# Chunk 0's triangular inverse made from 16x16 blocks joined on TensorE, in a DeltaNet and SiLU feed-forward kernel

## The chip, the cores and the metric

The kernel runs on one core of a Trainium2 chip. The metric is the device time of one execution in microseconds (us). The compute engines are PE (TensorE; its weight loads are shown apart as PEld), DVE (VectorE), ACT (ScalarE) and POOL (GpSimd); SP starts most of the DMAs. Each engine works through its own queue in order.

## What is computed

The reference is a DeltaNet recurrence per batch and head, followed by a two-layer network with SiLU. Everything is float32; batch 4, 8 heads, 768 tokens, head size 48, feed-forward size 2048.

```python
k_n = k / (norm(k) + 1e-6)
for t in range(S):
    y[:, :, t] = einsum('bhd,bhde->bhe', q[:, :, t], state)
    v_old = einsum('bhde,bhd->bhe', state, k_n[:, :, t])
    state = state + beta_t * einsum('bhd,bhe->bhde', k_n[:, :, t], v_t - v_old)
x = y.transpose(0, 2, 1, 3).reshape(3072, 384)
h = x @ w_in                      # 384 x 2048
out = (h * sigmoid(h)) @ w_out    # 2048 x 384
```

## The kernel before

The 768 tokens are cut into six chunks of 128 tokens (`c`), each into two halves of 64 (`hf`). All 32 (batch, head) pairs of a chunk are worked on together, in two groups of two batches (`g`). Within a half, the token-by-token recurrence becomes matrix work: scores between keys, a triangular matrix that has to be inverted, and products with the state.

For each chunk, `turn` (L395) transposes keys (`j` = 0) or negated queries (`j` = 1) on PE into `kq`, `score` (L418) multiplies them into `ap`, and `block_out` and `block_in` (L461, L472) send the 32x32 diagonal blocks of the key scores to DRAM and read them back as `g`, one block per partition: 4 quarters of the chunk times 32 pairs fill the 128 partitions. `norm_steps` (L328) makes the key norms and the factors that `block_steps` (L372) turns into the table `step`.

`invert` (L480) then inverts the 128 triangular blocks on DVE. For m from 31 down to 1 it forms a rank-1 term and adds it: two operations in each of 31 rounds, 62 in all, over 31 to 256 elements in a partition. For chunk 0 (`by_rows`), ACT scales finished rows and turns part of the result while DVE goes on. The result `x`, and half of it transposed (`low`), go to DRAM, from where `xe` and `xi` are read in the layout that `merge` needs, one pair's rows on 32 partitions. `merge` (L556) joins two 32x32 inverses to a 64x64 one with 32x32 matmuls. `solve` (L716) goes on with `keys`, `inner`, `update`, `old` and `new`: products with keys, states, values `vf` and queries, which write the layer input `xT` and the state (L632). Chunk 0's first half has no state yet and takes `first_outputs` (L640) with a slab in `sums_of_w`.

The feed-forward part (`feed_forward`, L913) for a half chunk is `hidden` (L764: 8 steps of f, two column tiles each; PE L771, SiLU on ACT L781) and, for chunk 0, `project` (L794, PE L801). From chunk 1 on `combine` (L855) does the second product with seven half-size products (PE L867), with sums of halves of the weights (`sum_w`) and of the activations (`sum_g`, L851); DVE adds partial results to the output tile (L875).

The weights arrive as float32 words that `narrow` (L176) rounds to a short form before use. There are 16 pieces, eight of `w_in` and eight of `w_out`, 768 KB each. Each takes two ACT operations (L180, L181), then on DVE a maximum (L185), a shift and mask (L188) and a combination with the sign (L192), and an add on POOL (L196). `w_in` pieces are 3 rows of 256 elements in a partition, `w_out` pieces 2 of 384. Raw pieces are parked in tiles not yet in use: `w_outs`, `sums_of_w`, `sums_of_g`, buffers of `gT`.

No scheduler decides the order: `pin` (L78) keeps each engine's instructions in the order in which the code emits them, and `in_line` (L88) does so for SP's DMAs. `run` (L1069) emits the next step of the feed-forward part (first narrowing, with `until`, whatever that step needs), `fill` (L942) the next narrowing step, and `go` the next step of another generator. `busy` (L281) emits matmuls whose result nobody uses (`pw`).

Around the change the order is: keys of chunk 0 loaded, turned, scored, blocks out and back; then queries and weights loaded; chunk 0's inversion on DVE with the query work of chunk 0, key turning of chunk 1 and the first narrowing ACT steps beside it (L1013 to L1033); scaling of V by the norms and masking of the query scores on DVE (L389, L1037); turning of chunk 1's queries (L408); then `solve(0)` with `fill` between its steps, the second half of chunk 0 together with the first hidden pass, `prepare(1)`, and chunk 1's inversion with narrowing and projection between its operations (L1152 to L1156). From there on the loop over chunks 1 to 5 solves a chunk, loads and prepares the next one and inverts its blocks, with feed-forward steps between.

Of the kernel before, what the change touches and what calls it, by code (L numbers as in the profile page):

```python
# [10 lines left out]
FP32 = mybir.dt.float32  # L11
# [10 lines left out]
def kernel(  # L22
# [13 lines left out]
    P = 128  # L36
# [131 lines left out]
    for hf in range(2):  # L168
        in_line(nc.sync.dma_start(out=beta_fm[BH // 2 : BH, :, 1 - hf], in_=of_beta[1][:, :, hf]))
    w_in = const.tile([P, NKT, DFF], FP32, name="w_in")  # L170
# [5 lines left out]
    def narrow(to, raw):  # L176

        low, high = raw[..., 0], raw[..., 1]
        bits = to.bitcast(U32)
        pin(nc.scalar.activation(out=to, in_=high.bitcast(FP32), func=ACTF.Abs))  # L180
# [5 lines left out]
            out=to, in0=to, scalar1=LOW_HIGH, scalar2=None, op0=ALU.max  # L186
        ))
        yield pin(nc.vector.tensor_scalar(  # L188
            out=bits, in0=bits, scalar1=3, scalar2=0x3FFFFFFF,
# [31 lines left out]

    def spare_w(i):
        return sums_of_w[i].rearrange("p f m -> p (f m)").bitcast(U32)

    def fetch_w_in(i):
        if i < 4:
            raw = room(1 - i // 2, i % 2)
        elif i == 4:
            raw = spare_w(2)
        elif i < NWI - 1:  # L230
            raw = mlp.tile([P, SIZE], U32, name="raw", tag="gT", bufs=3)[:]
        else:
            raw = spare
# [8 lines left out]
    def fetch_w_out(i):  # L242
        raw = (
            room(1, 0), room(1, 1), spare_w(1), spare_w(0), spare_w(2), room(1, 1), spare, spare_w(1)
# [31 lines left out]
    for j in range(NB):  # L276
        rows = slice(T * j, T * (j + 1))
        pin(nc.gpsimd.tensor_copy(out=pick[rows], in_=ident[rows, rows]))
    xis = [const.tile([P, HH, W], FP32, name=f"xi{i}") for i in range(2)]
# [48 lines left out]
    def norm_steps(c):  # L328
# [25 lines left out]
        for j in range(NB):  # L354
            rows = slice(T * j, T * (j + 1))
            yield pin(nc.vector.scalar_tensor_tensor(
                out=spread[rows, place(j), :], in0=r[rows], scalar=-1.0, in1=t[rows],
# [8 lines left out]
    def place(j):  # L366

        return 2 * (1 - j % 2) + j // 2
# [14 lines left out]
    def size(c, g):  # L383
# [4 lines left out]
        engine = nc.vector if c == 0 else nc.gpsimd  # L388
        pin(engine.tensor_tensor(out=vf, in0=vf, in1=of, op=ALU.mult))  # L389
# [60 lines left out]
    def block_room(c):  # L450

        blocks[c] = (
            tc.dram_tile([P, T, T], FP32, name=f"blocks{c}"),
            work.tile([P, T, T], FP32, name="g", tag="g", bufs=1),
            work.tile([P, T, T], FP32, name="x", tag="x", bufs=1),
        )
        x = blocks[c][2]
        pin(nc.gpsimd.memset(x[:], 0.0))
        pin(nc.gpsimd.memset(x[:].rearrange("p s t -> p (s t)")[:, 0 : T * T : T + 1], 1.0))

    def block_out(c, g):  # L461

        there, ap = blocks[c][0], aps[c, g]
        for j in range(NB):
            rows, cols = slice(T * j, T * (j + 1)), slice(T * (j % 2), T * (j % 2 + 1))
            at = T * place(j) + HH * g
# [5 lines left out]
    def block_in(c):  # L472
        there, g, _ = blocks[c]
        in_line(nc.sync.dma_start(out=g[:], in_=there[:]))
# [5 lines left out]
    def invert(c, step, by_rows):  # L480
# [3 lines left out]
        if by_rows:  # L484
            low = w_in[:, 0, DFF - T * T : DFF].rearrange("p (t s) -> p t s", t=T)
        else:
            low = g

        def turn_rows(engine, s):
            engine(low[EVEN, :, s], x[EVEN, s, :].rearrange("p s t -> p t s"))  # L490

        def scale_rows(s):
            n = s.stop - s.start
            pin(nc.vector.tensor_tensor(
                out=x[:, s], in0=x[:, s],
                in1=step[:, s].unsqueeze(2).to_broadcast([P, n, T]), op=ALU.mult,
            ))

        K = T // 4
        for m in range(T - 1, 0, -1):  # L500
# [8 lines left out]
            if by_rows and m >= K:  # L509
                pin(nc.scalar.activation(  # L510
                    out=x[:, m, m:T], in_=x[:, m, m:T], func=ACTF.Copy, scale=step[:, m : m + 1]
                ))
                if m in (T // 2, K):
                    turn_rows(by_act, slice(m, 2 * m))
# [707 lines left out]
```

## Time and profile before

| | us |
|---|---|
| median of 3 runs | 790.88 |
| lowest and highest run | 786.69, 790.92 |
| profiled execution | 791.45 |
| its span from first to last instruction | 789.70 |
| PE busy | 710.0 |
| PEld busy | 611.6 |
| DVE busy | 414.0 |
| ACT busy | 201.4 |
| POOL busy | 79.0 |

Busy time is a sum over the span; the same number can hide a stage in which an engine is full and one in which it stands still. So the profile is read by stage. A line such as L504 is a line of the code above; "out<-in" names the tiles; `x62` counts records (a float32 matmul of PE leaves two). "[1.68 <-DMA w]" gives idle time of the engine before the instruction and what ended it. PEclk is the TensorE clock that was granted, as a share of full speed. A list of waits gives the waiting operation, what it waited for, the time in total, how many times and the longest.

### The profile page before, as it was taken

How to read it: one execution, taken by the hardware profiler on the slowest of the kernel's cores; microseconds unless marked ns; L12 is line 12 of the kernel's file. 1: busy time of each engine (PE TensorE's matmuls, PEld its weight loads, DVE VectorE, ACT ScalarE, POOL GpSimd, SP SyncE). 2: the span in 40 equal slices, each digit the busy share in tenths (PEclk: the TensorE clock that was granted, in tenths of full speed). 3: DMA queues.
4: the chain of work that ended last, by engine and by line, in shares of the span. 5: the costliest groups of instructions: out<-in, count | busy, mean ns of one | idle time of the engine just before them, and what ended most of it. 6: DMA issues, size and time to landing. Idle time of an engine off the chain costs nothing.

```text
span 789.7 us, 19980 instructions
## 1 busy us (share of the span) xinstructions
PE 710.0 (90%) x8762; PEld 611.6 (77%) x8762; DVE 414.0 (52%) x969; ACT 201.4 (26%) x423; POOL 79.0 (10%) x82
## 2 busy tenths in 40 slices
PE   5667679688998999998989999989999989999997
PEld 3445566357767888997878998888997978989997
DVE  5868957994503395542395543495443494321212
ACT  2544235203202303212302213202213203222020
POOL 5002514300000100100100100100102000000000
PEclk9579889879999999999999999999999999999999
DMA  5997337004006704018504018404017204010000
GB/s 100 250 149 243 120 79 153 35 21 82 12 21 85 101 1 92 14 30 99 86 0 94 14 29 105 80 22 81 10 28 89 54 21 81 11 29 5 21 1 21
DMA packets 155655, 50.75 MB, mean 64 GB/s; under 512 B 141216, under 2 KB 148512, under 8 KB 155568
## 3 DMA queue, kind: packets, MB, share of 16 engines
q1 hardware_dynamic: 151200, 48.42, 32.7%
q10 hardware_dynamic: 4368, 1.05, 0.7%
q8 instruction: 69, 1.13, 0.6%
q14 instruction: 18, 0.15, 0.1%
HBM read 34.70 MB, written 12.58 MB: 60 GB/s over the span
## 4 chain that ended last, share of the span: by engine, by line
PE 54%; DVE 20%; DMA 9%; issue 2%; ACT 2%; SPq 1%; POOL 0%; DVEq 0%; ACTq 0%
PE phid L771 18%; PE px L867 8%; PE py L867 7%; DVE rank L504 7%; DVE x L515 6%; PE pa L428 3%; PE pyc L681 3%; DMA z<-in_q_dram 3%; PE po L801 3%; PE ph L595 2%; PE pz L607 2%; PE pu L627 2%; PE pyc L668 2%; DMA g<-blocks 2%; PE pt L402 2%
## 5 line engine op out<-in xcount | busy, mean ns | idle before, releaser
L771 PE MATMUL phid<-xT,w_in 128*128 128x256 f32 x1152 | 270.6, 389 | 4.5 <-ACT gT L781 2.8
L771 PEld LDWEIGHTS phid<-xT,w_in 128*128 128x128 f32 x1152 | 217.4, 193 | 40.4 <-issue 3.8
L781 ACT ACTIVATE gT<-phid 128x512 f32<-128x512 f32 x96 | 57.2, 597 | 219.9 <-PE phid L771 213.3
L504 DVE SCALAR_TENSOR_TENSOR rank<-g,step,x 128x31 f32<-128x31 f32 (+15 forms) x186 | 74.6, 401 | 31.2 <-DMA g<-blocks 25.9
L515 DVE TENSOR_TENSOR x<-x,rank 128x31 f32<-128x31 f32 (+15 forms) x186 | 68.3, 367 | 6.8
L867 PE MATMUL py<-w_out,sums_of_g 128*128 128x192 f32 x320 | 58.9, 337 | 7.9 <-DVE o L875 7.9
L867 PEld LDWEIGHTS py<-w_out,sums_of_g 128*128 128x128 f32 x320 | 53.7, 195 | 9.6 <-DVE o L875 9.1
L801 PE MATMUL po<-w_out,gT 128*128 128x384 f32 x128 | 48.4, 535 | 12.8 <-POOL w_out L196 11.4
L851 DVE TENSOR_TENSOR sums_of_g<-gT 128x384 f32<-128x384 f32 (+1 forms) x60 | 29.3, 511 | 54.8 <-ACT gT L781 44.2
L867 PE MATMUL px<-sums_of_w,sums_of_g 128*128 128x192 f32 x320 | 55.3, 326 | 0.0
L867 PEld LDWEIGHTS px<-sums_of_w,sums_of_g 128*128 128x128 f32 x320 | 52.6, 190 | 0.0
L801 PEld LDWEIGHTS po<-w_out,gT 128*128 128x128 f32 x128 | 25.8, 207 | 33.9 <-POOL w_out L196 15.4
L438 DVE TENSOR_TENSOR ap<-pa,above 128x256 f32<-128x256 f32 x40 | 15.1, 419 | 62.2 <-ACT ap L443 60.0
L446 DVE COPY xT<-pyc 32x128 f32<-32x128 f32 (+2 forms) x66 | 18.7, 284 | 45.1 <-ACT xT L443 45.1
L607 PEld LDWEIGHTS pz<-vf,xi 64*64 64x64 f32 x768 | 38.2, 134 | 4.5 <-issue 2.0
L607 PE MATMUL pz<-vf,xi 64*64 64x48 f32 x768 | 41.0, 216 | 0.5 <-DVE vf L600 0.5
L318 POOL TENSOR_TENSOR sq<-kb 128x384 f32<-128x384 f32 x24 | 19.7, 842 | 205.5 <-PE px L570 136.6
L595 PE MATMUL ph<-state,kq 48*64 48x48 f32 x704 | 30.4, 224 | 7.6 <-DVE state L632 7.6
L595 PEld LDWEIGHTS ph<-state,kq 48*64 48x64 f32 x704 | 27.4, 138 | 12.3 <-DVE state L632 8.0
L668 PE MATMUL pyc<-kq,state 48*64 48x64 f32 x704 | 35.0, 223 | 0.0
L668 PEld LDWEIGHTS pyc<-kq,state 48*64 48x64 f32 x704 | 32.1, 134 | 3.2 <-issue 3.2
L428 PE MATMUL pa<-kq 48*64 48x128 f32 (+1 forms) x896 | 30.1, 281 | 3.1 <-ACT kq L412 2.8
(142 smaller groups left out, 860.8 us busy)
## 6 DMA issues: line engine op xcount, KB each, us to landing
vf<-in_v_dram SPq DMA_DIRECT2D x24, 192.0 KB, 5.6
out_dram<-o SPq DMA_DIRECT2D x48, 96.0 KB, 2.2
g<-blocks SPq DMA_DIRECT2D x6, 512.0 KB, 3.6
w_out<-in_moe_w_in_dram SPq DMA_DIRECT2D x4, 768.0 KB, 7.6
sums_of_w<-in_moe_w_out_dram SPq DMA_DIRECT2D x4, 768.0 KB, 5.8
blocks<-ap SPq DMA_DIRECT2D x44, 64.0 KB, 2.2
xi<-up SPq DMA_DIRECT2D x44, 64.0 KB, 2.8
up<-x SPq DMA_DIRECT2D x5, 512.0 KB, 4.1
```

Source lines behind the costliest of these rows:

```text
L428: pin(nc.tensor.matmul(pa[e][half, p * n * W : (p + 1) * n * W], lhsT=kq[rows, p, 0, half], rhs=kq[rows, p, js[0] : js[-1] + 1, half], sta ...
L504: pin(nc.vector.scalar_tensor_tensor(out=tv, in0=g[:, 0:m, m : m + 1].to_broadcast([P, m, n]), scalar=step[:, m : m + 1], in1=x[:, m : m + ...
L515: yield pin(nc.vector.tensor_tensor(out=x[:, 0:m, m:T], in0=x[:, 0:m, m:T], in1=tv, op=ALU.add))
L595: yield pin(nc.tensor.matmul(ph[on(e, hf), n * D : (n + 1) * D], lhsT=kqs[c, g * HB + u][of, p, 0, on(e, hf)], rhs=states[g][of, u, p, 0:D ...
L607: yield pin(nc.tensor.matmul(pz[rows, n * D : (n + 1) * D], lhsT=xis[g][rows, u * H + 2 * p + e, :], rhs=vfs[c][rows, hf, g * HB + u, p, : ...
L668: yield pin(nc.tensor.matmul(py[to, C * p + W * u : C * p + W * (u + 1)], lhsT=states[g][of, u, p, :], rhs=kqs[c, g * HB + u][of, p, 1, on ...
L681: yield pin(nc.tensor.matmul(py[to, C * p + W * u : C * p + W * (u + 1)], lhsT=zbuf[rows, g * HB + u, hf, p, :], rhs=aps[c, g][rows, 1, u, ...
L771: pin(nc.tensor.matmul(ph[:, j * GT : (j + 1) * GT], lhsT=w_in[:, a, (2 * f + j) * P : (2 * f + j + 1) * P], rhs=xTs[c, hf][:, a, :], star ...
L781: pin(nc.scalar.activation(out=gTs[f // FG][:, f % FG, :], in_=ph[:], func=ACTF.Silu, scale=0.5))
L801: pin(nc.tensor.matmul(po[n][:, 0:DM], lhsT=gTs[f // 2 // FG][:, f // 2 % FG, at : at + C], rhs=w_outs[f // HFF][:, f % HFF, :], start=(f ...
L851: pin(nc.vector.tensor_tensor(out=sums_of_g[:, k, fs], in0=of[0], in1=of[1], op=op))
L867: pin(nc.tensor.matmul(to, lhsT=at, rhs=quarter(f, *b) if isinstance(b, tuple) else sums_of_w[b][:, f], start=start and f == 0, stop=f == ...
```

## The change

1. Chunk 0 no longer uses `invert`. `invert_first` treats each 32x32 block as two diagonal 16x16 blocks (`corners`) that are inverted side by side: 15 rounds of two DVE operations over 30 to 128 elements, with a scaling before and after. Two VectorE transposes of 32x32 blocks change the layout from one block per partition to one pair's rows on 32 partitions, so nothing of chunk 0's inverse goes through DRAM. PE joins the 16x16 parts in three sets of matmuls (pl): 128 of 32x32 by 16 columns, and 64 and 128 of 32x32 by 32, with evacuations by DVE and ACT between. Narrowing steps (`fill`) stand between these steps.
2. In `narrow`, L185 and L188 address their elements crosswise: the outer index is the element of a row, the inner one the row (256x3 or 384x2 in place of 3x256 or 2x384). The same elements are written.
3. Narrowing pieces are parked in other places, and ACT's part starts for the next two pieces in the queue. Chunk 1's inversion starts only when all pieces are narrow; before, pieces stood between its operations.
4. Chunk 0's queries are loaded right after beta and are turned and scored before and beside the start of the inversion. From chunk 1 on the loads of Q, V and K, which were issued one after the other, stand in three places: Q after the last state update, V in the preparation, K in the inversion of the next chunk.
5. V of chunk 0 is scaled on POOL, not DVE. The masks of chunk 0's query scores come after the merges, chunk 1's keys are turned in `solve(0)` and its queries in `prepare(1)`, by ACT and not DVE.
6. In `combine`, one partial result goes through a tile `kept` that ACT writes; DVE adds it at the end. The number of feed-forward steps between inversion operations changes.

The core of the diff:

```diff
+    load_q(0)
...
+        across = "p a f -> p f a"
...
         yield pin(nc.vector.tensor_scalar(
-            out=to, in0=to, scalar1=LOW_HIGH, scalar2=None, op0=ALU.max
+            out=to.rearrange(across), in0=to.rearrange(across), scalar1=LOW_HIGH, scalar2=None, op0=ALU.max
         ))
         yield pin(nc.vector.tensor_scalar(
-            out=bits, in0=bits, scalar1=3, scalar2=0x3FFFFFFF,
+            out=bits.rearrange(across), in0=bits.rearrange(across), scalar1=3, scalar2=0x3FFFFFFF,
             op0=ALU.logical_shift_left, op1=ALU.bitwise_and,
         ))
...
-        engine = nc.vector if c == 0 else nc.gpsimd
-        pin(engine.tensor_tensor(out=vf, in0=vf, in1=of, op=ALU.mult))
+        done = pin(nc.gpsimd.tensor_tensor(out=vf, in0=vf, in1=of, op=ALU.mult))
...
+    def invert_first(step):
+
+        x = blocks.pop(0)[2]
+        g2, x2 = corners(AT_G), corners(AT_X)
+        of = step[:].rearrange("p (i m) -> p i m", i=2)
+        yield pin(nc.vector.tensor_tensor(
+            out=g2, in0=g2, in1=of.unsqueeze(2).to_broadcast([P, 2, Q, Q]), op=ALU.mult
+        ))
+        for m in range(Q - 1, 0, -1):
+            n = Q - m
+            t = work.tile([P, T * T // 4], FP32, name="rank1", bufs=1)
+            tv = t[:, 0 : 2 * m * n].rearrange("p (i s t) -> p i s t", i=2, s=m)
+            shape = [P, 2, m, n]
+            pin(nc.vector.tensor_tensor(
+                out=tv, in0=g2[:, :, 0:m, m : m + 1].to_broadcast(shape),
+                in1=x2[:, :, m : m + 1, m:Q].to_broadcast(shape), op=ALU.mult,
+            ))
+            yield pin(nc.vector.tensor_tensor(
+                out=x2[:, :, 0:m, m:Q], in0=x2[:, :, 0:m, m:Q], in1=tv, op=ALU.add
+            ))
+        yield pin(nc.vector.tensor_tensor(
+            out=x2, in0=x2, in1=of.unsqueeze(3).to_broadcast([P, 2, Q, Q]), op=ALU.mult
+        ))
...
+        pin(nc.vector.transpose(out=low.rearrange("p n s -> p s n"), in_=x[:, 0:Q, :]))
...
+        pin(nc.vector.transpose(
+            out=up.rearrange("p n t -> p t n"), in_=x.rearrange("p s t -> p t s")
+        ))
...
+        for n in range(BH):
...
+                pin(nc.tensor.matmul(
+                    pl[rows[j], Q * n : Q * (n + 1)], lhsT=aps[0, g][rows[j], 0, nn // H, nn % H, cols],
+                    rhs=low[rows[j], n, :], start=True, stop=True,
+                ))
...
+            pin(nc.vector.scalar_tensor_tensor(
+                out=y[:, of, 0:Q], in0=pl[:, of], scalar=second[:],
+                in1=pick[:, 0:Q].unsqueeze(1).to_broadcast([P, HH, Q]), op0=ALU.mult, op1=ALU.add,
+            ))
...
-        add_half(o[:, 0, left], py[:, right])
+        pin(nc.scalar.mul(kept[:], py[:, right], 0.5))
...
+        pin(nc.vector.tensor_tensor(out=o[:, 0, left], in0=o[:, 0, left], in1=kept[:], op=ALU.add))
...
+                for next_up in list(queue)[:2]:
+                    if next_up.name in raws:
+                        next_up.begin()
...
+    inv = invert_first(step)
+    for n in range(1 + Q):
+        done = next(inv)
+        if n in (4, 7, 10, 13):
+            busy(1, done, Sync)
...
+    fill(4)
+    go(inv)
+    fill(3)
+    go(inv)
+    fill(1)
+    go(inv)
...
-    inv = invert(1, step, False)
-    for n in range(18):
-        go(inv, 2)
-        run()
-        fill(1)
-    go(inv, 99)
+    while queue:
+        run()
+        fill(2)
+    load_k(2)
+    inv = invert(1, step)
+    for n, _ in enumerate(inv):
+        if n % 4 != 3:
+            run()
...
-            for n, _ in enumerate(invert(c + 1, step, False)):
-                if n % 10 not in (2, 5, 8):
+            for n, _ in enumerate(invert(c + 1, step)):
+                if n % 7 != 3:
                     run()
-            run(8)
+                if n == 3:
+                    load_k(c + 2)
+            run(9)
```

## The prediction

> **What bounds the kernel now.** I read the page's slices first, then busy time by stage, then PE's waits, then the timeline of the weight narrowing. Each digit of the slices is 19.7 us.
>
> ```profile
> span 789.7 us, 19980 instructions
> ...
> PE   5667679688998999998989999989999989999997
> ...
> DVE  5868957994503395542395543495443494321212
> ...
> PEclk9579889879999999999999999999999999999999
> ```
>
> After the ninth slice PE is nearly always busy, so the end is the moment at which PE becomes continuously supplied, plus the matrix work left then. Only the first 190 us have much to give. By stage (columns: PE, PEld, DVE, ACT, POOL busy; granted clock; DMA share; GB/s):
>
> ```profile
> 20.58:45.82 25.24, 12.55 (x156) 8.43 (x154) 23.10 (x62) 14.83 (x45) 0.00 (x0) 0.57 1.21 225
> 45.82:73.34 27.52, 24.92 (x535) 18.62 (x535) 18.43 (x28) 11.35 (x19) 2.50 (x2) 0.91 0.82 218
> 73.34:84.22 10.88, 3.27 (x23) 2.61 (x22) 10.71 (x11) 3.49 (x5) 5.85 (x4) 0.88 0.24 74
> 84.22:149.17 64.95, 53.13 (x577) 38.98 (x574) 49.22 (x82) 25.39 (x44) 26.90 (x18) 0.92 0.48 117
> 149.17:188.85 39.68, 28.41 (x88) 19.58 (x86) 33.75 (x67) 6.94 (x11) 3.77 (x2) 0.78 0.19 43
> 300.00:789.70 489.70, 468.86 (x5849) 426.10 (x5847) 217.42 (x553) 110.38 (x236) 22.04 (x24) 0.99 0.26 44
> ```
>
> The first row is chunk 0's inversion: DVE 23.1 of 25.2 us. In the third DVE is full (10.71 of 10.88) and PE works 3.27. In the fifth, the end of chunk 1's inversion, DVE has 33.75 of 39.68 and PE's clock is 0.78. From 300 us PE has 96%. PE's waits name the culprits:
>
> ```profile
> PE po L801 <- POOL w_out L196: 11.4, 5, 5.0
> PE pg L375 <- DVE spread L356: 10.6, 2, 5.9
> PE pt L402 <- DMA kb<-in_k_dram: 9.9, 2, 9.6
> PE py L867 <- DVE o L875: 7.9, 4, 2.5
> PE ph L595 <- DVE state L632: 7.6, 1, 7.6
> PE pt L402 <- DMA z<-in_q_dram: 6.9, 5, 2.3
> ```
>
> The first and fifth are weight narrowing: PE waits for narrowed w_out, or for a state update queued on DVE behind narrowing. Its rhythm:
>
> ```profile
> 78.77 0.96 DVE L192 SCALAR_TENSOR_TENSOR w_in<-w_out,w_in 128x768 uint32<-128x768 uint32 x1
> 79.64 0.69 DVE L185 TENSOR_SCALAR w_in<-w_in 128x768 f32<-128x768 f32 x1
> 79.86 1.89 POOL L196 TENSOR_TENSOR w_in<-w_in,w_out 128x768 int32<-128x768 int32 x1 [1.68 <-DMA w_out<-in_moe_w_out_dram]
> 80.36 1.94 DVE L188 TENSOR_SCALAR w_in<-w_in 128x768 uint32<-128x768 uint32 x1
> 82.33 0.96 DVE L192 SCALAR_TENSOR_TENSOR w_in<-sums_of_w,w_in 128x768 uint32<-128x768 uint32 x1
> 83.21 1.01 DVE L632 TENSOR_TENSOR state<-state,pu 128x384 f32<-128x384 f32 x2
> ```
>
> One piece takes 3.56 us (78.77 to 82.33). L188, 0.69 us by itself, takes 1.94: it ends 0.55 after POOL's L196, as if it had stood still while POOL ran. DVE sets the pace until all 16 pieces are narrow and chunk 1 is inverted; PE sets it after.
>
> I count between three checkpoints that both orders have. A: both chunk-0 state adds (L632) done, five w_in pieces through L192; before, 84.2. B: chunk 1's first merge matmul (L570); before, 188.85. Then the end.
>
> **To A, along DVE.** The inversion starts when the blocks have come back (before, 20.58) and the step table is copied (19.76). The Q load now stands on SP's queue ahead of the block stores. Its issues took 3.83 us; after the beta issues (end 6.54) they end near 10.4, before the first store is wanted (11.06), so SP delays nothing. Its 768 KB land some 4.4 us later, near 14.8, beside the stores: their cost is between 0 and the 4.4. PE and ACT do two query batches (2.87 us each in the trace) before the step table's matmul, so the table comes near 21.2. I start at 21.4, +0.8 (between 0 and +3.5).
>
> The 62 operations of 25.2 us, plus 0.42 scaling and 0.38 of copy, become 30 of 30 to 128 elements. From old rows of those sizes (multiply 0.27 to 0.36, add 0.20 to 0.29, 0.035 between): 4.8 + 3.8 + 1.05 = 9.7. Two scalings of 512 elements at 0.69 (L1037) make 11.1: 32.5.
>
> Two VectorE transposes, 512 and 1024 elements, have no row. A contiguous pass costs 1.08 ns, fixed 0.13, if w_out's 768 elements go two a pass (547 ns, 384 passes) and w_in's three rows as two beside one (685 ns, 512 passes). The strided copy g<-x (512 elements in 0.627) gives 1.93 ns if it takes two a pass. So 1.9 us without a stride penalty, 3.2 with; the patterns step 16 and 32 words like g<-x, so 3.1: 35.6. [...]
>
> Narrowing, now strided: L185 and L188 were 0.69 (w_in) and 0.55 (w_out). With g<-x's 1.93 ns over 384 passes they take 0.87. Bounds: 0.55 (no penalty) and 2.2 (one element a pass, 1.93 ns plus a second such penalty of 0.85 for writing). I take 0.87, the only strided row. Five pieces by 2 x 0.87 + 0.96: 13.5.
>
> Other DVE work to A: two L593 from PSUM 0.84; copies from PSUM for xes 1.38, xi 2.76, y 1.38, second merge 1.38; masks 2.5; z and sums 1.1; xT 1.1; states 1.1: 13.5. V's scaling (1.83) goes to POOL, as do the identity copy and clearing the slab (1.42); turning chunk 1's queries (2.6) goes to ACT. POOL was idle 48.5 us up to 65.12, and ACT's 14.8 us in the inversion lose the row scalings, so both have room; a second clearing of spread (POOL, 0.2) and the sum for `second` wait for nobody on this chain.
>
> Waits: POOL's add behind each piece cost L188 1.25; copies from PSUM now stand in between, so 0.5 each, 2.5; two round trips to PE, 2.5. A is 35.6 + 13.5 + 13.5 + 5 = **67.6, 16.6 earlier**. The joining matmuls (128, 64, 128 of 32x32; 2.2 us per 128 by L570) run beside the narrowing. Chunk 0's low, up, xe and xi transfers vanish: 12 DMAs, whose round trip was 8.2 (48.76 to 56.99). I count that nowhere else, since the DVE chain covers its place.
>
> **A to B, along PE.** Since merge(1) now comes after all of the second hidden pass and half of the second projection, PE's work up to it is: two hidden passes 47.8 (192 by 0.249), one and a half projections 36.3 (96 by 0.378), chunk 0's second half 11 (keys, inner, update, old, new: 1.0 to 1.2 for each group), query turns 2.5, scores 4.1: 101.7, less 3 done before A. Stalls: 6 (2 to 20). B = 67.6 + 98.7 + 6 = **172.3**. DVE alone would allow less: eleven pieces by 3.8 plus 14.4 other work (reductions 2.2, vf 1.1, norms 4.5, read 0.4, states 1.1, xT 1.7, masks 3.4) and 4 waits reach 128; inversion and scaling 25.5 (it no longer has narrowing among its operations), transfers 10.1: 163.7. So PE, 9 us later, sets B, and what hides chunk 1's inversion is PE's own work, as long as 0.87 holds.
>
> **B to the end.** Before: 789.7 - 188.85 = 600.85. At B before, 30 hidden matmuls (7.5) and the whole second projection (24.2) were open; now 12.1: 19.6 less. Later chunks: ACT empties py into kept, easing the 7.9 at L867 (one add of 192 elements, 0.35, extra on DVE); Q no longer shares its flight with K and V (6.4 of z waits after 200 us); each inversion carries 27 run steps instead of 22. V still goes ahead of the block stores; K goes behind the block read, where it can hold up only the next chunk's squares. Together -2 (-10 to +4): PE follows with its next wait. 172.3 + 600.85 - 19.6 - 2 = 751.5 of span; 1.75 lies around the span (791.45 - 789.70): **753**. The profiled execution is 0.6 above the median 790.88.
>
> **Rivals.**
> Cheap narrowing: strided operations no longer stand still behind POOL. A piece takes 2.7 to 2.9, A comes 2.5 earlier, stalls fall to 2; PE then sets everything: 746. For it: 1.25 of L188's 1.94 is waiting. Against: operands and result stay in SBUF as before, and no row shows a stride ending the wait. [...] Chance 0.10.
> Dear narrowing: one element a pass, 1.7 (1.93 ns). A piece is 4.36, 0.6 above my 3.75; sixteen are 10 us: 763, and with 2.2, 1.6 above, 26 us: 779. For it: g<-x shows that a stride costs. Against: the same row fits two elements a pass. Chance 0.14.
> Late supply: the shorter inversion is real but weights, Q or PSUM round trips come late, stalls 20 and start +3.5: 753 + 14 + 3 = 770. For it: DMA share 1.21 in the inversion and 5.62 us of ACT's waiting for a w_out transfer. Against: chunk 0's round trips of the inverse, some 1.5 MB, leave the queues. Chance 0.12.
> Slower: the strided L185 and L188 cost so much that DVE loses more than it gained. The gain is 38; over 16 pieces that is 2.4 a piece, so it turns at (3.75 + 2.4 - 0.96) / 2 = 2.6 us an operation; at 3.0 (both penalties and a step twice as dear as g<-x's) it gives 804. Against: 2.6 is four times the old mean alone. Chance 0.07, 0.06 of it beyond 1%.
>
> **How the numbers follow.** My case has 0.57: 753, by itself 742 to 765. The eight-in-ten range reaches from cheap narrowing and the -10 of the later chunks, 738, to dear narrowing and late supply, 778. About 1% is what a measurement of this kernel can tell from no change (783 to 799). Under 783 lie my case, cheap and late (0.79) and 0.09 of dear, whose far end is bounded by 779 before a late start is added: 0.88. The rest of dear and 0.01 of slower lie within 1%: 0.06. Slower by more: 0.06.
>
> **What would show it.** Right: about 30 short inversion operations ending near 32.5; transposes together near 3 us; strided L187 and L190 near 0.87 alone; A near 68, merge(1) near 172 with PE's idle time before it under 15 us; clock near full from 70 us on. Wrong: strided rows above 1.5; PE waiting for POOL's add over 10 us in the first projection; the first step table after 24; PE waits beyond 300 us larger than 21.

## The result and the profile after

The changed kernel takes 758.5 us (median of 4 runs, 757.6 to 760.1) where the kernel before takes 790.9 (786.7 to 794.7); the ratio is 0.959 with a 95% interval from 0.954 to 0.965. Its profiled execution took 760.12 us, with a span of 758.1. The prediction was 753, in a range from 738 to 778: the sign and the size of the whole are right. Its stages are not: two of them missed by 13 and 9 us in opposite directions.

The top of the page after, to be held against the four rows shown of before:

```profile
span 758.1 us, 21218 instructions
...
PE   5779996799999999999999999999999999999996
...
DVE  5856877997454493544593543593543593321212
...
PEclk9655999999999999999999999999999999999999
```

PE is full from the ninth slice on (a slice is now 19 us), and no later slice has an 8. The third and fourth slices, 38 to 76 us, have a clock digit of 5: this is where the prediction failed. The stages between its checkpoints (PE, PEld, DVE, ACT, POOL busy; granted clock; DMA share; GB/s), first after, then the two that were not shown of before:

```profile
21.38:31.83 10.45, 9.08 (x82) 6.08 (x83) 9.31 (x32) 6.66 (x16) 0.63 (x1) 0.50 0.96 265
31.83:80.69 48.86, 41.71 (x1161) 31.46 (x1161) 31.98 (x41) 18.38 (x28) 14.69 (x8) 0.64 0.44 128
80.69:187.91 107.22, 93.16 (x752) 69.13 (x750) 89.25 (x149) 35.37 (x60) 33.21 (x20) 0.97 0.42 95
187.91:758.10 570.19, 552.73 (x7177) 501.11 (x7176) 272.87 (x684) 136.42 (x298) 30.23 (x32) 1.00 0.27 47
```

```profile
84.22:188.85 104.63, 81.54 (x663) 58.56 (x659) 82.97 (x148) 32.33 (x54) 30.67 (x20) 0.87 0.37 89
188.85:789.70 600.85, 576.01 (x7239) 515.58 (x7238) 267.31 (x684) 134.96 (x291) 29.28 (x32) 0.99 0.27 45
```

The inversion itself takes 10.5 us instead of 25.2. Yet A (both state adds, five pieces of w_in) comes at 80.69, only 3.5 us earlier. From A to B (chunk 1's first merge matmul) the time is 2.6 us longer, but by the prediction's count 19.6 us more matrix work is done in it: worth 17.0. From B to the end it is 30.7 shorter, 19.6 of it that same work: worth 11.1. 3.5 + 17.0 + 11.1 = 31.6, the difference of the two spans. The rows put the moved work lower: the 30 hidden and 64 projection matmuls open at B before took 7.8 and 20.9 us, the 32 open there now 12.0. By this 16.7 us moved, and the last two stages are worth 14.1 and 14.0.

PE's waits after, for the list shown of before:

```profile
PE pa L438 <- ACT kq L422: 7.3, 5, 4.5
PE pt L412 <- DMA z<-in_q_dram: 6.7, 5, 1.4
PE po L877 <- POOL w_out L198: 5.5, 4, 1.8
PE pl L583 <- issue: 4.8, 1, 4.8
```

The wait for POOL's add of w_out fell from 11.4 to 5.5, those for spread, state and o are gone, and a stop of 4.8 us that is put down to "issue" (PE waited for nothing that the profile shows) stands in the first joining set. The kernel before had one of 1.4 us, in the products after its merges:

```profile
68.49 0.34 PE L651 MATMUL py<-ap,sums_of_w 64*64 64x64 f32 x6 [1.36 <-issue]
```

Where A went is seen in PE's timeline of the joins after (start, duration, instruction, and in brackets the idle time before it):

```profile
32.99 1.26 PE L583 MATMUL pl<-sums_of_w,ap 32*32 32x16 f32 x128
34.18 0.91 PE L294 MATMUL pw<-state,ident 128*128 128x384 f32 x2
35.02 0.48 PE L583 MATMUL pl<-sums_of_w,ap 32*32 32x16 f32 x34
40.30 1.47 PE L583 MATMUL pl<-sums_of_w,ap 32*32 32x16 f32 x94 [4.79 <-issue]
...
44.55 2.77 PE L603 MATMUL pl<-sums_of_w,sums_of_g 32*32 32x32 f32 x97 [0.21 <-issue]
...
50.20 1.59 PE L618 MATMUL pl<-sums_of_g,sums_of_w 32*32 32x32 f32 x99 [0.73 <-issue]
...
57.10 2.88 PE L650 MATMUL py<-sums_of_w,ap 32*32 32x32 f32 x101 [1.29 <-issue]
59.91 1.65 PE L294 MATMUL pw<-state,ident 128*128 128x384 f32 x2
```

The joins begin at 33 and the merges (py) at 54.9. Before, the merges began at 56.99, by way of DRAM. So an inversion that ends 14 us earlier (31.83 for 45.82) gives 2 us at the merges. Two things fill the joins: stops of 7.0 us in all, and the clock. Before the stop of 4.79 one pw, a matmul of two records, takes 0.91 us, after it 1.65. (`x128` is 128 records, so 64 of the float32 matmuls.)

### The profile page after: what moved, and what is told of

It is laid out like the page before. It is cut to its first block, busy times and chain, and to the rows that moved or that the text cites. A ratio compares the mean times of both kernels' runs of the same rounds, so it can differ in the third digit from the quotient of the medians.

```text
span 758.1 us, 21218 instructions
## 1 busy us (share of the span) xinstructions
PE 709.8 (94%) x9394; PEld 617.4 (81%) x9394; DVE 414.0 (55%) x942; ACT 203.8 (27%) x417; POOL 88.2 (12%) x86
## 4 chain that ended last, share of the span: by engine, by line
PE 70%; DVE 11%; DMA 4%; issue 1%; POOL 1%; ACT 1%; SPq 0%; DVEq 0%; ACTq 0%; POOLq 0%
PE phid L847 27%; PE px L944 14%; PE py L944 9%; PE pyc L761 3%; DMA z<-in_q_dram 3%; PE pa L438 3%; PE pu L707 2%; PE pyc L748 2%; PE ph L675 2%; PE pt L412 2%; PE po L877 2%; PE pz L687 2%; DVE w_out L190 2%; DVE rank L513 2%; DVE x L518 2%; PE px L650 1%
## 5 line engine op out<-in xcount | busy, mean ns | idle before, releaser
L847 PE MATMUL phid<-xT,w_in 128*128 128x256 f32 x1152 | 263.3, 384 | 0.0
L513 DVE SCALAR_TENSOR_TENSOR rank<-g,step,x 128x31 f32<-128x31 f32 (+15 forms) x155 | 62.2, 401 | 28.5 <-DMA g<-blocks 24.0
L927 DVE TENSOR_TENSOR sums_of_g<-gT 128x384 f32<-128x384 f32 (+1 forms) x60 | 32.7, 567 | 58.0 <-ACT gT L857 47.3
L944 PE MATMUL px<-sums_of_w,sums_of_g 128*128 128x192 f32 x320 | 58.2, 331 | 0.0
L518 DVE TENSOR_TENSOR x<-x,rank 128x31 f32<-128x31 f32 (+15 forms) x155 | 54.7, 353 | 5.7
L944 PE MATMUL py<-w_out,sums_of_g 128*128 128x192 f32 x320 | 55.3, 326 | 0.0
L877 PE MATMUL po<-w_out,gT 128*128 128x384 f32 x128 | 46.0, 505 | 5.5 <-POOL w_out L198 5.5
L687 PEld LDWEIGHTS pz<-vf,xi 64*64 64x64 f32 x768 | 39.8, 141 | 9.3 <-issue 7.1
L687 PE MATMUL pz<-vf,xi 64*64 64x48 f32 x768 | 42.6, 224 | 4.5 <-DVE nt L354 3.8
L877 PEld LDWEIGHTS po<-w_out,gT 128*128 128x128 f32 x128 | 23.7, 194 | 22.5 <-POOL w_out L198 8.0
L438 PEld LDWEIGHTS pa<-kq 48*64 48x64 f32 x896 | 23.7, 147 | 14.0 <-ACT kq L422 9.0
```

The costliest lines, as they stand in the source:

```text
L438: pin(nc.tensor.matmul(pa[e][half, p * n * W : (p + 1) * n * W], lhsT=kq[rows, p, 0, half], rhs=kq[rows, p, js[0] : js[-1] + 1, half], sta ...
L513: pin(nc.vector.scalar_tensor_tensor(out=tv, in0=g[:, 0:m, m : m + 1].to_broadcast([P, m, n]), scalar=step[:, m : m + 1], in1=x[:, m : m + ...
L518: yield pin(nc.vector.tensor_tensor(out=x[:, 0:m, m:T], in0=x[:, 0:m, m:T], in1=tv, op=ALU.add))
L687: yield pin(nc.tensor.matmul(pz[rows, n * D : (n + 1) * D], lhsT=xis[g][rows, u * H + 2 * p + e, :], rhs=vfs[c][rows, hf, g * HB + u, p, : ...
L847: pin(nc.tensor.matmul(ph[:, j * GT : (j + 1) * GT], lhsT=w_in[:, a, (2 * f + j) * P : (2 * f + j + 1) * P], rhs=xTs[c, hf][:, a, :], star ...
L877: pin(nc.tensor.matmul(po[n][:, 0:DM], lhsT=gTs[f // 2 // FG][:, f // 2 % FG, at : at + C], rhs=w_outs[f // HFF][:, f % HFF, :], start=(f ...
```

## The experiments

Each is the changed kernel with one edit unless said otherwise, timed in three rounds against the kernel before on its own chip. Ratios are to the kernel before; the changed kernel's is 0.959 [0.954, 0.965].

### Row-by-row narrowing

```diff
-            out=to.rearrange(across), in0=to.rearrange(across), scalar1=LOW_HIGH, ...
+            out=to, in0=to, scalar1=LOW_HIGH, ...
...
-            out=bits.rearrange(across), in0=bits.rearrange(across), scalar1=3, ...
+            out=bits, in0=bits, scalar1=3, ...
```

> The changed kernel with the maximum (L187) and the shift (L190) addressed row by row again, as before the change; nothing else differs. Theory: the crosswise addressing only costs. Alone these operations went from 0.69 to about 0.93 us, and beside POOL's add they still stand (2.3 us for L190 of w_out), so a back-to-back piece takes 4.2 us where it took 3.56. With row-by-row addressing a piece should come back to about 3.6, the second inversion should start some 6 us earlier than 151.8, and the kernel should be 2 to 8 us faster than the changed one (about 751 to 757). Rival 1: the addressing ends part of the mutual standing still of VectorE and POOL, and going back makes the stretch from 80 to 152 us longer and the kernel slower than 758. Rival 2: PE sets the pace there anyway, the narrowing ends earlier and the end does not move (within 1 us of 758).

Measured: 753.05 us, ratio 0.951 [0.949, 0.954], 5.5 us faster. Two pieces back to back, first of the changed kernel, then of this one:

```profile
138.24 0.96 DVE L194 SCALAR_TENSOR_TENSOR w_out<-sums_of_w,w_out 128x768 uint32<-128x768 uint32 x1
139.12 0.97 DVE L187 TENSOR_SCALAR w_out<-w_out 128x768 f32<-128x768 f32 x1
140.13 2.32 DVE L190 TENSOR_SCALAR w_out<-w_out 128x768 uint32<-128x768 uint32 x1
142.48 0.96 DVE L194 SCALAR_TENSOR_TENSOR w_out<-sums_of_w,w_out 128x768 uint32<-128x768 uint32 x1
```

```profile
130.82 0.96 DVE L193 SCALAR_TENSOR_TENSOR w_out<-sums_of_w,w_out 128x768 uint32<-128x768 uint32 x1
131.69 0.55 DVE L186 TENSOR_SCALAR w_out<-w_out 128x768 f32<-128x768 f32 x1
132.28 2.08 DVE L189 TENSOR_SCALAR w_out<-w_out 128x768 uint32<-128x768 uint32 x1
134.40 0.96 DVE L193 SCALAR_TENSOR_TENSOR w_out<-sums_of_w,w_out 128x768 uint32<-128x768 uint32 x1
```

From sign to sign a piece takes 4.24 us crosswise and 3.58 row by row. POOL's add runs beside both (from 139.43 for 2.19 us, from 132.01 for 1.94). L190, which takes 0.95 alone, still takes 2.32: the crosswise form does not end the standing still beside POOL, it lengthens both operations. B comes at 178.7 instead of 187.9. The theory holds; this part of the change costs 5 us.

### Chunk 0 inverted in whole blocks again

```diff
-    inv = invert_first(step)
...
     load_v(0)
...
     for i in (3, 4):
         fetch_w_in(i)
     load_k(1)
...
+    fetch_w_in(5)
+    inv = invert(0, step)
+    for n in range(T - 1):
+        done = next(inv)
+        if n % 6 == 5:
+            busy(1, done, Sync)
+    go(inv)
...
+    fill(9)
```

> The changed kernel with chunk 0 inverted in whole 32x32 blocks by the routine of the later chunks, with the layout changed by way of DRAM, and not in 16x16 blocks joined on TensorE; the loads of V, the fourth to sixth pieces and chunk 1's keys are issued ahead of it, narrowing, resizing of V and the clearing of the slab come after it. Theory: the block inversion ends 16 us earlier on VectorE, but its three joining sets, run at a clock of 0.50 with a stop of 4.8 us, give the 16 us back: chunk 0's first merge began at 54.9 us where it began at 57.0 before the change. Then this kernel loses only what VectorE cannot narrow meanwhile, and is 0 to 8 us slower (758 to 766). Rival, by the prediction's own sum (16.6 us earlier to checkpoint A by the inversion): 770 to 778.

Measured: 759.8 us, ratio 0.960 [0.955, 0.964], no different from the changed kernel. PE around the first merge in this run:

```profile
45.62 1.62 PE L294 MATMUL pw<-state,ident 128*128 128x384 f32 x2 [2.57 <-DVE sums_of_w L518]
54.64 0.31 PE L653 MATMUL py<-sums_of_w,ap 32*32 32x32 f32 x2 [7.40 <-DMA sums_of_w<-low]
55.59 3.62 PE L653 MATMUL py<-sums_of_w,ap 32*32 32x32 f32 x126 [0.64 <-DMA sums_of_w<-low]
```

Its merges start at 54.64, the changed kernel's at 54.87. The part that the change is named for, blocks of 16, VectorE's transposes and three joining sets, cannot be measured in the time: the transfers through DRAM it saves are replaced by an equally long chain of PE, ACT and DVE. The three narrowed pieces that follow in a row here (49.9, 52.7, 57.5) catch up with what the joins had let through (38.3, 43.5, 58.0). The first merge runs at half clock here too (3.62 us for 126 records, where before 128 took 2.21), so this run does not tell what either way would be worth at full clock.

### Narrowing between the operations of chunk 1's inversion

```diff
-    while queue:
-        run()
-        fill(2)
     load_k(2)
     inv = invert(1, step)
-    for n, _ in enumerate(inv):
-        if n % 4 != 3:
-            run()
+    for n in range(15):
+        go(inv, 2)
+        run()
+        if n % 2 == 0:
+            run()
+        fill(1 + n % 2)
+    go(inv, 99)
```

> The changed kernel in which chunk 1's inversion starts before the last pieces are narrow, and narrowing and feed-forward steps stand between its operations, as before the change (two operations, then one or two feed-forward steps and one or two narrowing steps); nothing else differs. From checkpoint A to B the changed kernel does 19.6 us more matrix work in 2.6 us more: PE idles 14.1 us there where it idled 23.1, and the clock is 0.97 where it was 0.87. Theory: that comes from narrowing all pieces first, since PE then does not wait for POOL's add of w_out (11.4 us before, 5.5 after, the longest 5.0 and 1.8) nor loses the clock behind such waits. Then these waits grow here to 9 us or more, and the kernel is 6 to 16 us slower (764 to 775). Rival: VectorE has the same sum of work either way, the inversion ends as late as it did and PE has other work beside it; then within 3 us of 758.5, and the gain of that stretch comes from the keys and queries of chunk 1 being turned elsewhere.

Measured: 772.2 us, ratio 0.974 [0.971, 0.978], 13.7 us slower. The wait that the theory named is back, larger than before the change:

```profile
PE po L877 <- POOL w_out L198: 14.7, 4, 7.6
```

This wait is 9.2 us longer than in the changed kernel, and PE's idle time from A to B grows by as much (23.3 us for 14.1); the clock there is 0.92 for 0.97. So narrowing every piece before the second inversion is one of the two parts that earn the gain. The counts of steps are not those of before to the letter (15 rounds, not 18, with more steps in each), so the 13.7 us are the price of this mix.

### The steps in the later inversions, the loads, and the tile kept

```diff
-                if n % 7 != 3:
+                if n % 10 not in (2, 5, 8):
                     run()
...
-            run(9)
+            run(8)
```

> The changed kernel with the old numbers of feed-forward steps in the inversions of chunks 2 to 5: 22 of 31 operations followed by a step, and 8 steps after them, in place of 27 and 9. Theory 2: before the change PE waited for VectorE's add into o (7.9 and 1.7 us) because more inversion operations stood on VectorE between two feed-forward steps; then these waits come back here and the stretch after chunk 1's first merge goes from 570 to 575 to 581, the kernel to 763 to 769. Theory 1 (the loads apart): within 3 us of 758.5. If neither this nor the loads move it by 3 us, what is left is the queries of later chunks emptied by the activation engine instead of VectorE, and the order of the preparation.

Measured: 772.4 us, ratio 0.976 [0.971, 0.980], 13.9 us slower. From B to the end it takes 582.3 us instead of 570.2, and PE waits for VectorE again:

```profile
PE phid L847 <- DVE o L952: 10.0, 7, 2.9
```

With fewer feed-forward steps between them, more inversion operations stand on DVE ahead of the add into o, and PE's next product waits for the bank that this add empties. PE's idle time after B grows by 7.6 us (25.1 for 17.5). The other 4.5 of the 12.1 are longer busy time of the same 7177 records, which is not explained. This is the other part that earns the gain.

```diff
         if hf == 1 and g == 1:
             load_q(c + 1)
+            if c > 0:
+                load_k(c + 2)
...
         if c + 1 < NCH:
+            load_v(c + 1)
...
-                if n == 2:
-                    load_v(c + 1)
...
-                if n == 3:
-                    load_k(c + 2)
```

> The changed kernel with the loads of Q, V and K of chunks 2 to 5 issued together again after the last state update, as before the change; nothing else differs. After chunk 1's first merge the changed kernel takes 570.2 us where 581.3 us were left by the matmuls open; taking the tile kept out did not move that (570.1). Theory 1: the loads apart bring the 11 us; then the stretch after the first merge of chunk 1 goes to some 575 to 581, with more PE waits for z, and the kernel to 763 to 769. Theory 2: the feed-forward steps between the inversion's operations bring it; then this kernel is within 3 us of 758.5.

Measured: 759.4 us, ratio 0.959 [0.954, 0.964]. B to end takes 570.7. Issuing the loads apart is worth nothing that can be measured; after B the wait for z is 6.2 us together and 5.3 apart.

```diff
-        kept = mlp.tile([P, HM], FP32, name="kept", bufs=1)
...
-        pin(nc.scalar.mul(kept[:], py[:, right], 0.5))
+        add_half(o[:, 0, left], py[:, right])
...
-        pin(nc.vector.tensor_tensor(out=o[:, 0, left], in0=o[:, 0, left], in1=kept[:], op=ALU.add))
```

> The changed kernel with the partial product of combine added by VectorE straight from py, as before the change, without the tile kept; nothing else differs. Theory: most of the 11 us that the changed kernel gains after chunk 1's first merge comes from kept, because PE's wait for VectorE's add into o (7.9 and 1.7 us before) is gone with it. Then this kernel loses 7 to 10 us (about 766 to 768) and the wait of py for o is back among PE's waits. Rival: the gain comes from the loads of Q, V and K standing apart and from the other numbers of feed-forward steps between the operations of the inversion; then this kernel loses under 3 us.

Measured: 760.3 us, ratio 0.961 [0.957, 0.965]; B to end 570.1 against 570.2. My theory of that run fell, and the wait for o hardly came back: 0.5 us at py. (At pz, 2.5 us are put down to o and 1.3 to vf; the changed kernel has the same 3.8 there, put down to nt.) The tile kept neither gains nor costs.

### What lengthens the joins: loads in flight, and the clock

```diff
+    last = next(op for e, op in pins.items() if e == nc.tensor.engine)
     for i in (3, 4):
         fetch_w_in(i)
+        if i == 3:
+            behind(line[-1], last, Sync)
     load_k(1)
```

> The changed kernel in which the fourth piece of w_in, and behind it on the same queue chunk 1's keys and the fifth and later pieces, are issued only when PE has done the first set of joining matmuls (L583). Theory: PE's stop of 4.8 us in the midst of that set, put down to nothing but issuing, lies at a time at which the DMA engines were full with these loads, while PE's instructions come through a queue of the same engines; with the loads held back the stop should shrink to under 1 us, and the joining and A come 3 to 5 us earlier, if the later loads do not then make narrowing or chunk 1's keys late. Rival: the stop has nothing to do with the loads and stays at 4 to 5 us; then the kernel is the same or slower by what the late pieces cost (0 to 6 us).

Measured: 760.6 us, ratio 0.961 [0.958, 0.964], no gain. The stop moved: 1.2 us in the first set, but 2.3, 1.2, 0.5 and then 4.3 at py while the loads came.

```diff
-    for i in (3, 4):
-        fetch_w_in(i)
-    load_k(1)
-    for i in (5, 6):
-        fetch_w_in(i)
...
             merge(0, 0, False)
+            last = pins[nc.tensor.engine]
+            for i in (3, 4):
+                fetch_w_in(i)
+                if i == 3:
+                    behind(line[-1], last, Sync)
+            load_k(1)
+            for i in (5, 6, 7):
+                fetch_w_in(i)
             merge(0, 1, False)
```

> The changed kernel in which the fourth and later pieces of w_in and chunk 1's keys are issued only when PE has done the first half of chunk 0's first merge matmuls (L650), so that from some 37 us to there hardly any load is in flight; V's loads stay. In the run in which these loads were issued after the first joining set, PE's stops put down to issuing moved with them: 1.2 us in the first set (4.8 without the delay), then 2.3, 1.2, 0.5 and 4.3 us while the loads came. Theory: they lengthen wherever loads are in flight, and each stop costs more by taking the clock down to 0.50. Then the stops up to the merge are under 1 us each here, the clock stays above 0.8 through the joins, and checkpoint A comes 5 to 12 us earlier unless the fourth piece comes late; the kernel 748 to 757. Rival: the stops of about 1 to 4 us stay at the same instructions whatever is in flight, the clock stays at 0.50 and late pieces cost 2 to 6 us: 760 to 766.

Measured: 756.6 us, ratio 0.956 [0.951, 0.960]; the interval overlaps the changed kernel's, so the 1.9 us are not shown as a gain. Its joins:

```profile
37.17 1.47 PE L583 MATMUL pl<-sums_of_w,ap 32*32 32x16 f32 x94 [1.55 <-issue]
...
49.10 1.02 PE L618 MATMUL pl<-sums_of_g,sums_of_w 32*32 32x32 f32 x99 [0.79 <-issue]
...
52.55 2.17 PE L650 MATMUL py<-sums_of_w,ap 32*32 32x32 f32 x101 [2.00 <-issue]
```

With next to no loads in flight the first stop is 1.55 instead of 4.79 and the merges begin at 49.9, 5 us earlier. But the stops at L618 and L650 stay, so only the part above some 2 us belongs to the loads. A comes only 3 us earlier (77.7): 1.6 us go to longer stops behind the merges' start (2.00 for 1.29 at L650, and a new one of 0.84 at L687), and the clock is 0.50 from 56 to 68 us as in the changed kernel. Between theory and rival this run stands in the middle.

```diff
-        if n in (4, 7, 10, 13):
+        if n > 0:
             busy(1, done, Sync)
...
             if n % HH == HH - 1:
-                busy(1)
+                busy(4)
...
-            busy(1)
+            busy(2)
```

(busy(2) stands also after the second joining set and in place of busy(1) in the five steps of solve(0).)

> The changed kernel with more matmuls of no use (pw) on PE from 22 to 90 us: 14 instead of 4 beside the rounds of the inversion, and two to four instead of one between the joining sets. Theory: checkpoint A came at 80.7 instead of 67.6 for a good part because PE had a granted clock of 0.50 in the inversion and 0.64 from 32 to 81 us, so that the 32x32 matmuls and the query products of that stretch took about twice their time; with PE kept working the clock should be above 0.8 there, A 4 to 9 us earlier and the kernel 3 to 8 us faster (about 750 to 755). Rival: A is set by VectorE's own work and by PE's stops in issuing (4.8 us at 35.5 us); then the added matmuls only lie in the way and the kernel is the same or up to 5 us slower.

Measured: 767.4 us, ratio 0.972 [0.966, 0.978], 8.9 us slower. The clock rose (0.93 from 58 to 81 us, px in 2.63 us where it took 3.62), but the added matmuls were still running at 38.8 when the joins could begin at 33, and A came some 6 us later. That the half clock lengthens the products is seen in the rows; that it can be bought back with useless matmuls is not shown.

### Together

The first joins row-by-row narrowing and the late loads of the runs above.

> The changed kernel with both row-by-row narrowing (5.5 us faster by itself) and the fourth and later pieces of w_in and chunk 1's keys issued after the first half of chunk 0's first merge (1.9 us faster by itself). If the two act at different places, one on the length of a narrowing piece from 80 to 152 us and the other on the joins from 33 to 55 us, the gains add: 751 (749 to 753). If both only take slack from the same chain, the sum is that of the larger: 753.

Measured: 749.7 us, ratio 0.945 [0.942, 0.948]; B at 176.5. Beside the 5.5 us of the narrowing alone another 3.3 are there, as if the gains added, though the late loads were not shown as a gain by themselves.

```diff
-                    if next_up.name in raws:
+                    if next_up.name in raws and next_up.name not in (("out", 4), ("out", 5), ("out", 6), ("out", 7)):
...
         turn(0, b, 1, M)
+        if b > 1:
+            busy(1)
         score(0, b, (1,), (A, CC), evacuate)
```

> The kernel with row-by-row narrowing and late loads, and two things more: the activation engine no longer starts on the last four pieces of w_out two pieces ahead (in the changed kernel one such start stood 6.5 us at the head of its queue until POOL released the place, and PE waited 4.5 us for key and query copies behind it), and a matmul of no use (pw) between turning and scoring of the last two batches of chunk 0's queries, so that PE's clock is up when the joins begin at 33 us. Theory: the first removes the PE wait (2.2 us is left of it with row-by-row narrowing), the second lets part of the 32x32 matmuls from 33 to 70 us run at full clock; 744 to 750. Rival: the added matmuls lie in the way and the pieces begun late make VectorE wait: 751 to 756.

Measured: 747.4 us, ratio 0.943 [0.940, 0.947]: not told apart from the last. The wait for kq fell to 1.4 us, and the clock is up from 24 us on (0.99 to 28, 1.00 to 34), but it is back at 0.50 by 35, after PE had waited 2.1 us for DVE's transpose.

```diff
             if g == 1:
                 yield
-            busy(1)
...
-        busy(1)
+        if n > 2:
+            busy(1)
```

> The fastest kernel so far (row-by-row narrowing, late loads, late starts of the last pieces, two matmuls of no use among the queries) without the matmuls of no use between the joins and in the first three steps of solve(0), five in all, which took about 1.6 us each at half clock on PE's path from 43 to 66 us. Theory 1: the clock is 0.50 from 36 to 66 us with them anyway, so without them checkpoint A comes up to 7 us earlier and the kernel is 3 to 7 us faster (741 to 744). Theory 2: they are what brings the clock up again at about 68 us; without them it stays at 0.50 until the first hidden pass has run for some 15 us, the 48- and 64-column products before it take twice their time, and the kernel is the same or up to 6 us slower (747 to 753).

Measured: 745.9 us, ratio 0.945 [0.941, 0.950], on a chip on which the kernel before took 791.4. A comes 0.8 us earlier than in the last run, not 7. Theory 1 fails in its size, theory 2 in its reason: the clock came back between 67 and 68 us without these matmuls too. The three together-kernels, 746 to 750 us, beat both the changed kernel and the one before, and are not told apart among themselves.

## Why the prediction came out right, and where it was wrong

- Start and inversion: predicted 21.4 to 32.5, measured 21.38 to 31.83. Right as a whole and for the adds (0.19 to 0.29 us). The multiplies take as long as the adds, where the sum had 0.27 to 0.36, and the second scaling takes 0.98 where it had 0.69; the two errors partly offset each other.
- The two transposes: predicted 3.1, measured as below, 3.07. That is 1.8 ns an element of a partition for both (512 and 1024 elements), without the fixed 0.13 of the prediction's estimate.

```profile
31.87 1.06 DVE L571 STREAM_TRANSPOSE sums_of_w<-sums_of_w 128x512 f32<-128x512 f32 x1
32.79 2.01 DVE L575 STREAM_TRANSPOSE sums_of_g<-sums_of_w 128x1024 f32<-128x1024 f32 x1
```

- The strided operations: predicted 0.87 alone, measured 0.86 to 1.00. Right. That L190 would go on standing beside POOL was the forecast against "cheap narrowing", and it does (2.3 us for w_out).
- A at 67.6: wrong by 13.1 us, and the failing term is "waits 5". DVE's work from the inversion's end to A is 31.98 us where the sum had 30.1 (3.1 + 13.5 + 13.5). Half of the 5, 2.5 us, was for L188 standing beside POOL, which the profile counts as work; so work came out as forecast (31.98 for 32.6), and what failed is the 2.5 us for "two round trips to PE". VectorE's idle time there is 48.86 - 31.98 = 16.9 us, 13.5 of it put down to ACT's copies out of PSUM, which follow PE's products. The sentence "the joining matmuls run beside the narrowing" has the chain the wrong way round: DVE waited for ACT's copies of PE's products, and for PE. Three things were missed in that chain. I took L570's 2.2 us for 128 matmuls, but it is that of 128 records, 64 matmuls: the three sets have 640 records, not 320. At half clock 128 records of L603 took 3.8 us. And PE stopped 7.0 us for "issue". The 1.83 us of scaling V that went to POOL mostly came back: L187 and L190 of the first piece took 1.53 and 2.02 us while POOL scaled V (33.94 to 37.45), 1.7 more than alone.
- A to B: predicted 104.7 (98.7 of work and 6 of stalls), measured 107.2. PE was busy 93.2 and idle 14.1, so the work was overestimated and the stalls were mis-sized by 8. DVE ended narrowing at 152, not 128: it started 13.1 us late, worked 57.6 us where the sum had 56.2, and idled 13.7 where it had 4, 10.6 of it put down to ACT's copies (xT, ap). "DVE allows 163.7, PE sets B 9 us later" failed. Both chains start from the last narrowed piece: chunk 1's inversion follows it directly on DVE, and PE, which had waited for that piece, then works without a break up to B and waits 0.93 us more for the inverse:

```profile
156.67 20.99 PE L847 MATMUL phid<-xT,w_in 128*128 128x256 f32 x96
177.49 10.48 PE L877 MATMUL po<-w_out,gT 128*128 128x384 f32 x32
187.91 0.24 PE L650 MATMUL py<-xe,ap 32*32 32x32 f32 x2
189.07 2.21 PE L650 MATMUL py<-xe,ap 32*32 32x32 f32 x126 [0.93 <-DMA xe<-low]
```

So the end of narrowing on DVE set B: in the row-by-row run it came 9.4 us earlier (142.5) and B 9.2. The work was overestimated because at full clock a record of a hidden matmul took 0.22 us (20.99 over 96) and one of the projection 0.33 (10.48 over 32), where the sum had 0.249 and 0.378.

- B to the end: predicted 2 us better than the work moved, measured 11.1 by its count of the moved work and 14.0 by the rows. The term was mis-sized: the run counts, which stood as one clause in "-2 (-10 to +4)", are worth 12.1 by the experiment; kept and the loads, named ahead of them, give nothing.

The total came within 6 us because A's 13.1 and the 2.5 of the next stage stood against 9.1 too little at the end; that much of the agreement is luck. By the prediction's count the gain was to be 16.6 up to A, 19.5 from A to B and 2 behind it; it was 3.5, 17.0 and 11.1. By the experiments the new inversion carries nothing that could be measured (759.8 us without it), and the change is carried by two edits of order, each worth about 14 us: narrowing finished before the second inversion, and more feed-forward steps among the later inversions' operations. What earns the rest of the 32.4 plus the 5.5 that crosswise addressing costs, some 10 us if the effects add, was not taken apart: V scaled on POOL, chunk 0's queries loaded early, chunk 1's keys and queries turned elsewhere.

## What to carry to other kernels

Follow a shortened stage to the first instruction that uses its result before booking the saving: here the inversion ended 14 us earlier and the merge began 2 us earlier. When a chain of vector work is swapped for sets of many tiny matmuls, price those at the clock that the stage will have and with their stops, not at the row of a busy stage: here 128 records took 3.8 us at half clock where the row said 2.2, and 7.0 us of stops came on top. And where two engines share the work, count how many of one's operations stand ahead of the add that frees the other's bank: a changed interleaving was worth 13.9 us here, the new algorithm nothing that could be measured.

## What the runs showed of the hardware

PE stopped at the same few places in every kernel with the joins, for 0.2 to 5.5 us, with nothing on the page as a cause. In the changed kernel the queue of instructions moved, from 20 to 60 us (packets, MB, share of the DMA engines):

```profile
q8 instruction: 7, 0.11, 1.1%
```

That is some 16 KB a packet. This queue moved 74 packets in the whole run for PE's 18939 records (matmuls, weight loads and a few others), and 69 for 17672 in the kernel before, so 256 records a packet.

That the stops are waits for these packets is argued from the trace's records of single packets. Counted from the start, PE has 961, 1217, 1473 and 1985 records behind it when its four stops end, which lie 256 or 512 apart; 3, 4, 5 and 7 packets have landed, the last of them 1.4 to 1.7 us before. The stop of the kernel before is at 1473 records and 5 packets, too. So all five lie at 961 records plus a multiple of 256. In nine kernels, the changed one among them, the first stop comes with 94 records of the first joining set left, and lasts 1.0 to 5.5 us. In its whole run the changed kernel has four stops of over 0.2 us put down to "issue", against 74 packets, and all four lie in the joins and the first merge, where 128 records of 32x16 products with their weight loads pass in 1.26 us and a packet takes 0.96 to 1.16 us to move.

The long stop is read as a late packet: PE stops at 35.5, and the packet begins to move at 37.8, while the loads fill the DMA engines (a share of 0.98 from 35.5 to 40.3). With the loads held back it begins at 34.8, 0.9 us ahead of the stop, and the stop is 3.2 us shorter. That it waits behind the loads is argued from this.

The clock did not follow PE's being occupied alone. In the trace's own record it is 0.50 or 1.00 and never between: in the changed kernel 0.50 from 15.47 to 32.53 us, 1.00 to 39.36, 0.50 to 73.49, so other values are means. These stretches are 5, 2 and 10 times 3.41 us, and in this trace and that of the kernel before all stretches between the first change and the last are whole multiples of it. PE was busy without a break from 57.1 us on, and the clock stayed at 0.50 for 16 us (columns as in the stages above):

```profile
60.00:64.00 4.00, 4.00 (x96) 2.92 (x98) 2.03 (x3) 1.12 (x2) 0.93 (x1) 0.50 0.02 4
64.00:68.00 4.00, 4.00 (x70) 2.86 (x68) 2.89 (x5) 0.61 (x2) 0.00 (x0) 0.50 0.01 4
68.00:72.00 4.00, 4.00 (x54) 2.83 (x54) 2.72 (x5) 1.49 (x3) 0.00 (x0) 0.50 0.01 2
72.00:76.00 4.00, 4.00 (x107) 3.27 (x104) 2.94 (x4) 2.74 (x5) 1.85 (x1) 0.81 0.01 4
```

Of the 16.2 us to 73.3, 11.3 went to 32x32 and 64x64 products and 4.9 to pw. From 27.6 on, where PE did nothing but pw matmuls of 128x128, the clock rose after some 5 us (0.50 up to 32, 0.73 from 32 to 33). So of two stretches of unbroken PE work one saw the clock rise after some 5 us, the other after 16. Whether the small products are the reason was not tested by itself.
